# Attention outputs computed transposed, in halves and quarters of the array, in a fused attention and MLP kernel

## The chip, the cores and the metric

One core of a Trainium2 chip runs the whole kernel as one program. The core has five engines with their own instruction streams: TensorE (PE in the profile; its weight loads are shown apart as PEld), VectorE (DVE), ScalarE (ACT), GpSimd (POOL) and SyncE (SP), which issues the DMA transfers. TensorE reads SBUF and writes PSUM, which has eight banks of 512 float32 values in each of 128 partitions. The metric is the time of one execution in microseconds, as the median of several runs; the profile is of one execution.

## The reference

For 4 batches and 8 heads, 768 positions of 48 values:

```
f = 1 / (1 + exp(-f_logit))
for t in range(768):
    state = f[t][:, None] * state + outer(k[t], v[t])     # 48 x 48 per batch and head
    y[t]  = q[t] @ state
x = heads of y side by side                               # [4, 768, 384]
x = x + relu(layernorm(x) * g @ w_ch1) @ w_ch2            # 384 -> 1536 -> 384
x = x + (token MLP over the 768 positions, 768 -> 256 -> 768)
x = x + relu(x @ w_ch1') @ w_ch2'
```

The weights of the MLPs come as float64 and are converted on the chip.

## The kernel before, in words

**Attention in units.** The 768 positions are cut into 6 chunks of 128, and a chunk of one batch is a unit `n` (`c, b = divmod(n, 4)`): 24 units. The function `attention(n)` registers the steps of a unit as named pieces of work. Heads are kept in 4 pairs `p`; the head `r` of a pair (0 or 1) lies in partitions 0 to 47 or 64 to 111 of a tile of 112 (`rows(r)`). The steps, with their names in the order:

- `lt` or `lf`, `lq`, `lv`: the DMA loads of q, k, f and of v; `clamp`, `log`, `scan`, `ek`, `eq`, `qm`, `km`, `tot`: the decay's logarithm, its running sum over the chunk, its exponentials, and q and k multiplied by them.
- `kp`, `kt`: k transposed on TensorE (line 297), and copied out by ScalarE.
- `sc`: the scores, K by Q, for each head with 48 rows of the array (line 312), into the two banks of the PSUM pool `scp`, one for each `r`. `A0`, `A1`: VectorE masks them into SBUF (line 320).
- `y0`, `y1`: the outputs, two pairs of heads each. For every pair one product of Q, 112 x 128, as weights with the carried state of two heads (`state[b]`, 112 x 96 per pair, the two heads' blocks on a diagonal) as 96 moving columns (line 332), if there is a carried state (c > 0); and for every head one of the masked scores, 128 x 128, as weights with V as 48 moving columns (line 335). The result is [128 positions, 384], in a bank of the pool `atp` (three banks).
- `st`: what the chunk adds to the state, for each head 48 columns of the transposed k as weights and 48 of V (line 346); `ste`: VectorE adds it to the state in two instructions, one for each `r` (line 357; ScalarE copies it when c = 0); `std`: GpSimd multiplies the state by the decay (line 350).
- `lna`: ScalarE copies y to `x` with a running sum (line 365); `lnc`, `tp`, `ah`, `al`, `lnv`, `lnr`: the layer norm's product, the transposes (line 418) and their split into a high and a low part, the norm's factor.

**The MLP work around it.** Three units make a step of the first MLP, `mlp(step, ...)`: twelve groups `m<step>.<f>` of nine matmuls of 384 columns (line 449) and twelve groups `m<step>.o<u><g>` of nine (line 479), with ReLU on ScalarE (`h`) and the low part on VectorE (`l`). The weights are loaded (`w<i>.ld`, 384 KB of int32 pairs each), converted by three VectorE instructions (`.a`, `.b`, `.c`) and split (`.h`, `.l`).

**What sets the order.** Each piece has a slot number, and TensorE pieces (`sl.p`) of a slot come behind the others (`sl.e`). Units 9 and later are 8 slots apart, and pieces from slot 77 on are issued by slot: attention first within a slot, then a group of nine matmuls. Pieces of the first 77 slots are issued in an order written out by hand, `ORDER`. An entry such as `0.kp+8` puts 8 matmuls on zeros (256 columns, bf16, `busy`, line 412) ahead of that piece. `POOL` names the pieces that run on GpSimd rather than VectorE. Within an engine the order of issue is the order of execution as written.

After the attention the token MLP and the second channel MLP follow, and last a check of the ranges of the inputs that chooses whether `general_path` runs; here it doesn't run.

Of the kernel before, what the change touches and what calls it, by code (L numbers as in the profile page):

```python
# [7 lines left out]
F32 = mybir.dt.float32  # L8
# [48 lines left out]
    2.lnr 1.al 4.kp w4.b 3.lna 5.lt m0.0 w3.a w2.a 4.kt 3.lnc w2.b 3.tp 4.A0 4.st 3.std 3.ah 5.lv 3.lnv 3.al
    4.y0 4.tot w2.c w3.b w2.h 4.y1 5.clamp w3.c 5.log w2.l m0.1 6.lt w4.c m0.h0 5.scan w4.h 4.lna m0.2 m0.l0
    w4.l 5.ek 4.ste 6.lv 5.eq 5.km m0.4 m0.h2 m0.h1 4.lnc w3.h 5.qm 5.kp m0.h4 w3.l 4.tp 5.kt 5.sc w5.a 4.ah
    m0.l1 5.tot 4.lnv w5.b m0.3 5.A0 4.std 5.A1 0.lnr 4.al 5.y0 m0.h3 w5.c m0.l3 1.lnr w5.h m0.l4 5.y1 w5.l  # L60
    m0.l2 w12.a 5.st 5.lna 7.lt 3.lnr m0.5 w12.b 5.lnc w12.c 5.tp m0.h5 5.ste 4.lnr 5.ah 7.lv 5.lnv 5.al
    5.std w17.ld m0.l5 w12.h m1.0+10 w14.a w13.ld w12.l m1.3 m1.h0 w14.b m1.l0 5.lnr m1.2 w17.a m1.h3 w14.c
    w13.a w14.h w21.ld w13.b m1.4 m1.h2 m1.l3 w14.l w15.ld m1.l2 w13.c m1.1 w17.b w13.h m1.h4 w13.l m1.l4
    m1.5 m1.h1 w15.a w17.c w15.b w17.h m0.o00 m1.l1 m1.h5 w17.l m1.l5 w15.c m0.o20 w16.a w15.h w16.b w16.c
    m0.o10 w15.l w9.ld w16.h w16.l w6.ld 6.clamp m0.o01 w21.a 6.log w21.b w10.ld w21.c m0.o11 6.scan w7.ld
    w21.h w11.ld w9.a 6.ek m0.o21 w21.l m0.r11 6.eq m0.r01 6.qm m1.o00 m0.r21 6.km w11.a 6.kp 6.tot m1.o20
    6.kt w11.b w11.c w9.b w11.h 6.st w11.l m1.o10 w9.c w10.a w20.ld w9.h w9.l m1.o21 w7.a w6.a w6.b m1.o11
    w6.c m1.r21 w8.ld w6.h w6.l 6.sc m1.r11 w10.b m1.o01 6.A1 6.A0 w10.c 6.y0 m1.r01 w10.h w23.ld w10.l m0.6
    w8.a w7.b w8.b m1.9 w8.c m0.h6 m0.l6 w8.h w8.l m1.6 m1.h9 7.clamp 7.log m1.l9 w7.c m0.8 w22.ld m1.h6
    7.scan w7.h w18.ld m1.l6 m1.8 w7.l m0.h8 7.ek m0.l8 7.eq 7.km m1.7 m1.h8 7.qm w20.a m1.l8 7.tot 7.kp  # L70
    m1.h7 w20.b 6.y1 7.kt w20.c w22.a w19.ld w20.h w22.b m0.9 6.lna w20.l 8.lt 6.lnc m0.10 w22.c m0.h9 w23.a
    w22.h w19.a m1.l7 w22.l 7.sc m0.h10 8.lv m0.l9 w19.b s0.ld m0.11 7.A0 w19.c 7.A1 8.clamp w19.h m1.10
    m0.h11 6.ste w19.l 8.log m0.l10 m0.l11 7.y0 6.std m1.h10 8.scan 7.st 7.y1 m1.l10 8.ek w18.a 8.eq 8.km
    6.tp 7.ste 9.lt 7.lna m0.7 6.lnv 8.qm 7.lnc 8.kp 6.ah w18.b 7.tp 8.kt 8.sc 6.al 9.lv 8.tot 7.ah w18.c
    7.lnv 7.al 7.std 8.st m0.h7 8.A0 m1.11 w18.h 7.lnr 8.A1 w18.l m0.l7 8.y0 9.clamp m1.h11 m1.l11 6.lnr
    9.log m0.o02 w23.b 9.scan m0.o12 w23.c 9.ek w23.h s1.ld 9.km m0.o22 9.eq w23.l 9.qm m0.o03 s0.a 9.tot
# [885 lines left out]
```

## Time and profile before

| what | value |
|---|---|
| median of 3 runs | 811.01 us (809.0 to 811.43) |
| the profiled execution | 809.86 us, of which the span from the first to the last instruction is 808.0 us |
| granted TensorE clock over the span | 0.992 |
| TensorE busy | 798.2 us in 5314 matmul instructions |
| VectorE, ScalarE, GpSimd busy | 408.3, 318.1, 212.7 us |
| end of the last output of attention | 393 us |

Busy time is a union of instructions, and those of TensorE overlap, so a share near 100% is to be read together with the times at which instructions start. The granted clock is a share of 2.4 GHz. Times in the timeline are microseconds from the start of the span.

### The profile page before, as it was taken

The page shows a single profiled execution, that of the slowest core. Times are in us where ns is not written, and L with a number is a line of the kernel's source. Part 1 is how long each engine was busy: PE and PEld are TensorE (multiplying, and loading weights), DVE is VectorE, ACT ScalarE, POOL GpSimd, SP SyncE. Part 2 cuts the span into 40 slices and gives each one's busy share as a digit, 9 for nine tenths or more (in the row PEclk, how much of TensorE's full clock was granted, in tenths as well). Part 3 has the DMA queues.
Part 4 walks back from the last instruction along what each step waited for, and adds up shares of the span by engine and source line. Part 5 has one row for each costly group of instructions (what it writes and reads, how often), then busy time and mean ns, then how long its engine had stood idle before and what let it go on. Part 6 is the DMA issues. An engine that isn't in the chain of part 4 may idle for free.

```text
span 808.0 us, 13517 instructions
## 1 busy us (share of the span) xinstructions
PE 798.2 (99%) x5314; PEld 780.8 (97%) x5314; DVE 408.3 (51%) x757; ACT 318.1 (39%) x797; POOL 212.7 (26%) x271
## 2 busy tenths in 40 slices
PE   8999999999999999999999999999999999999996
PEld 7899999999999999999999999999999999999996
DVE  6798896554645655546353352534334343524130
ACT  6664363432433423324043362534434353525020
POOL 4543054333333333322003451111112111212000
PEclk9799999999999999999999999999999999999999
DMA  9535453334544443352152463234333343332000
GB/s 239 203 105 168 118 165 96 124 113 151 147 123 143 119 136 113 118 176 85 40 157 85 130 197 106 79 99 128 108 99 95 101 128 108 82 95 69 30 2 33
DMA packets 42841, 93.19 MB, mean 115 GB/s; under 512 B 4800, under 2 KB 25408, under 8 KB 42768
## 3 DMA queue, kind: packets, MB, share of 16 engines
q1 hardware_dynamic: 42768, 92.23, 38.5%
q8 instruction: 44, 0.72, 0.4%
q14 instruction: 29, 0.24, 0.1%
HBM read 76.48 MB, written 15.73 MB: 114 GB/s over the span
## 4 chain that ended last, share of the span: by engine, by line
PE 96%; DMA 1%; ACT 1%; POOL 0%; issue 0%; SPq 0%; DVE 0%; DVEq 0%; POOLq 0%
PE mo L479 38%; PE mm L449 37%; PE y L335 5%; PE rt L640 3%; PE ht L664 3%; PE sc L312 3%; PE y L332 2%; PE tp L418 2%; PE st L346 1%; DMA first<-in_qkf_t 1%; PE kp L297 1%; DMA xr<-x_d 0%; PE kp L412 0%; POOL first L286 0%; SPq L249 0%
## 5 line engine op out<-in xcount | busy, mean ns | idle before, releaser
L449 PE MATMUL mm<-ah,w1h 128*128 128x384 f32 x576 | 198.0, 344 | 0.2 <-ACT xn L376 0.2
L479 PE MATMUL mo<-w2h,hh 128*128 128x384 f32 x576 | 197.4, 343 | 0.0
L449 PE MATMUL mm<-ah,w1l 128*128 128x384 f32 x576 | 193.1, 335 | 0.0
L479 PE MATMUL mo<-w2h,hl 128*128 128x384 f32 x576 | 193.0, 335 | 0.0
L449 PE MATMUL mm<-al,w1h 128*128 128x384 f32 x576 | 192.8, 335 | 0.0
L479 PE MATMUL mo<-w2l,hh 128*128 128x384 f32 x576 | 192.8, 335 | 0.0
L468 DVE SCALAR_TENSOR_TENSOR hl<-mm,hh 128x384 fp32r<-128x384 f32 x192 | 106.3, 555 | 141.6 <-ACT hh L464 141.4
L464 ACT ACTIVATE hh<-mm 128x384 fp32r<-128x384 f32 x192 | 94.0, 490 | 210.6 <-PE mm L449 210.2
L449 PEld LDWEIGHTS mm<-ah,w1h 128*128 128x128 f32 x576 | 108.2, 188 | 1.7 <-ACT xn L376 0.4
L479 PEld LDWEIGHTS mo<-w2h,hh 128*128 128x128 f32 x576 | 108.2, 188 | 1.6
L449 PEld LDWEIGHTS mm<-al,w1h 128*128 128x128 f32 x576 | 108.3, 188 | 0.2 <-DVE al L435 0.2
L479 PEld LDWEIGHTS mo<-w2l,hh 128*128 128x128 f32 x576 | 108.3, 188 | 0.1
L479 PEld LDWEIGHTS mo<-w2h,hl 128*128 128x128 f32 x576 | 108.1, 188 | 0.0
L449 PEld LDWEIGHTS mm<-ah,w1l 128*128 128x128 f32 x576 | 108.1, 188 | 0.0
L718 POOL TENSOR_TENSOR cs<-cs 128x384 f32<-128x384 f32 x56 | 47.3, 846 | 222.6 <-DVE cs L715 183.4
L435 DVE TENSOR_TENSOR al<-tp,ah 128x384 fp32r<-128x384 f32 x48 | 26.6, 553 | 50.9 <-ACT ah L431 50.8
L431 ACT ACTIVATE ah<-tp 128x384 fp32r<-128x384 f32 x48 | 23.4, 488 | 66.9 <-PE tp L418 66.4
L509 DVE TENSOR_TENSOR xr<-mo,xr 128x384 f32<-128x384 f32 x24 | 13.4, 557 | 68.9 <-PE mo L479 68.9
L335 PE MATMUL y<-V,A 128*128 128x48 f32 x336 | 47.8, 266 | 0.0
L498 DVE SCALAR_TENSOR_TENSOR x<-mo,rs,x 128x384 f32<-128x384 f32 x30 | 18.3, 617 | 55.8 <-PE mo L479 55.8
L335 PEld LDWEIGHTS y<-V,A 128*128 128x128 f32 x336 | 44.1, 191 | 0.3 <-DVE A L320 0.2
L261 POOL TENSOR_SCALAR T<-T 112x512 f32<-112x512 f32 x18 | 27.2, 1513 | 55.1 <-DMA T<-in_qkf_t 55.1
(135 smaller groups left out, 1044.9 us busy)
## 6 DMA issues: line engine op xcount, KB each, us to landing
cs<-in_w SPq DMA_DIRECT2D x48, 384.0 KB, 3.2
sg<-in_w SPq DMA_DIRECT2D x44, 384.0 KB, 3.7
T<-in_qkf_t SPq DMA_DIRECT2D x21, 672.0 KB, 5.3
f_d<-cu SPq DMA_DIRECT2D x32, 192.0 KB, 1.9
wf<-f_d SPq DMA_DIRECT2D x32, 192.0 KB, 2.5
x_d<-x SPq DMA_DIRECT2D x24, 192.0 KB, 1.9
xr<-x_d SPq DMA_DIRECT2D x24, 192.0 KB, 3.3
out<-xr SPq DMA_DIRECT2D x24, 192.0 KB, 1.9
```

The costliest lines, as they stand in the source:

```text
L261: eng("clamp").tensor_scalar(f, f, -43.0, None, op0=ALU.max)
L312: nc.tensor.matmul(t["sc"][r][:, p], t["K"][rows(r), p, :], t["Q"][rows(r), p, :])
L335: nc.tensor.matmul(y[:, D * h:D * h + D], weight(h), v[:, D * h:D * h + D], start=(c == 0), stop=(c == 0 or h % 2 == 1))
L431: nc.scalar.activation(out=ah, in_=src, func=AF.Copy)
L435: nc.vector.tensor_tensor(al, src, ah.bitcast(F32), op=ALU.subtract)
L449: nc.tensor.matmul(ps, w[:, f, k, :], x[:, k, :], start=(i == 0), stop=(i == 8))
L464: nc.scalar.activation(out=hid(f)[0], in_=t[f], func=AF.Relu)
L468: nc.vector.scalar_tensor_tensor(hl, t[f], 0.0, hh.bitcast(F32), op0=ALU.max, op1=ALU.subtract)
L479: nc.tensor.matmul(ps, x, w[:, f, :], start=(f == lo and i == 0), stop=(f == hi and i == 2))
L640: nc.tensor.matmul(t["r"][j][:, :DM], w[:, s, js], t[x, s], start=(s == 0 and i == 0), stop=(s == NCH - 1 and i == 2))
L664: nc.tensor.matmul(ps[:, :DM], w[:, j, js], x[:, j], start=(i == 0), stop=(i == 5))
L718: nc.gpsimd.tensor_tensor(t["u"], t["u"], t["h"], op=ALU.subtract)
```

## The change

Each head's output is computed transposed, [48 values, 128 positions], with what was moving as weights and what was weights as moving columns:

- `outp` takes two PSUM tiles from `scp`, the pool of the scores, one for each `r`. The head with `p % 2 == 0` writes partitions 0 to 63 and that with `p % 2 == 1` partitions 64 to 111, so that two heads lie in the halves of the array's columns. The products with the state use 48 rows at partition 0 or 64 and 64 or 48 columns, a quarter of the array, with Q as 128 moving columns; the products with V use all 128 rows and half of the columns, with the masked scores as 128 moving columns.
- `outp_e` copies the two tiles to SBUF on ScalarE (`yc0`, `yc1`); `outp_t` turns them back by four transposes on TensorE (`yt`) into the bank that `lna` reads.
- The state is stored as 48 columns for each pair, 112 x 192 and no longer 112 x 384; `ste` is one instruction, and `std` works on half as much.
- `st` uses 64 weight columns for the head in the lower half, and moves one slot ahead; `lna` and what follows it move one slot back.
- The heads are dealt out to pairs by `head(p, r)`; the layout on the host and the general path follow.
- `ORDER` and `POOL` are written anew. The matmuls on zeros in `ORDER` are 89, where they were 41: before `0.kp+8 0.y0+3 2.kp+5 3.kp+10 3.y0+5 m1.0+10`; after `0.kp+6 0.sc+9 0.y+6 1.kp+7 1.st+8 1.y+4 0.tp+3 1.tp+3 2.sc+9 2.y+7 2.yt+4 4.y+5 5.y+6 m0.3+12`. In units 4 to 7 it keeps `st` and `y` apart.

```diff
 POOL = set("""
-    1.qm w0.l 2.km 3.clamp w4.l w5.l w12.l 4.clamp w13.l 4.qm w14.l w17.l w7.l 6.qm w19.l w21.l 8.clamp
-    w22.l w23.l 8.km 9.clamp 10.clamp
+    2.clamp 2.qm w2.l w3.l w4.l 4.clamp 4.km w15.l 5.clamp w16.l w6.l w8.l w9.l w19.l 7.km w21.l 9.clamp
+    9.qm 9.km 10.clamp
 """.split())
 ORDER = """
-    0.lf 1.lf 0.lq 0.clamp 0.log 2.lf 1.clamp 1.log 1.lq 0.scan 1.scan 0.ek 1.lv 0.eq 0.km 1.ek 0.lv 1.eq
-    0.qm 0.kp+8 3.lt 0.kt 1.km 0.sc 2.clamp 1.qm 2.log 1.kp 0.A0 0.st 0.A1 2.lq 0.ste 1.tot 0.y0+3 2.scan
-    1.kt 0.tot 2.ek 4.lt 0.y1 3.clamp 2.eq 2.tot 3.log 1.sc 2.qm 0.lna 2.km 1.st 1.A1 2.lv 1.ste 1.A0 w0.ld
...
+    0.lf w0.ld 1.lf 0.lq 0.clamp 0.log w0.a w0.b 2.lf 0.scan 0.lv 1.clamp 0.ek 1.lq w0.c 0.eq 0.km w0.h
+    1.log 0.tot 0.kp+6 w0.l 3.lt 0.qm 0.kt 1.scan 0.sc+9 0.st 2.clamp 1.ek 0.A1 w2.ld 1.eq 0.A0 0.ste 1.lv
+    1.tot 0.y+6 1.qm 2.log 2.lq 3.clamp 1.km 0.yc0 0.yc1 2.scan 1.kp+7 3.log 2.lv 1.sc w5.ld w2.a 2.ek
+    3.scan 0.yt 2.eq w15.ld 1.kt 2.km 3.ek 1.st+8 w14.ld 1.A1 0.std 3.eq 2.kp 1.A0 0.lna 4.lt 2.qm 1.y+4
...
 """.split()
+def head(p, r):
+
+    return 4 * (p // 2) + 2 * r + p % 2
...
-    state = [s1.tile([P2, NP, 2 * D], F32, name=f"state{b}") for b in range(B)]
+    state = [s1.tile([P2, NP * D], F32, name=f"state{b}") for b in range(B)]
...
-        def outp(g, z=0):
-            if g == 0:
-                t["y"] = atp.tile([128, 512], F32, tag="at", name="y")
-                busy(t["y"], z)
-            y = t["y"]
-            v = t["V"]
-            for p in (2 * g, 2 * g + 1):
-                if c:
-                    nc.tensor.matmul(y[:, 96 * p:96 * p + 96], t["Q"][:, p, :], state[b][:, p, :],
-                                     start=True, stop=False)
-                for h in (2 * p, 2 * p + 1):
-                    nc.tensor.matmul(y[:, D * h:D * h + D], weight(h),
-                                     v[:, D * h:D * h + D], start=(c == 0), stop=(c == 0 or h % 2 == 1))
+        def outp(z=0):
+
+            t["yT"] = [scp.tile([128, NP, 128], F32, tag="sc", name="yT") for _ in range(2)]
+            busy(t["yT"][0].rearrange("p a c -> p (a c)"), z)
+            heads = [(p, r, slice(64 * (p % 2), 64 * (p % 2) + (D if p % 2 else 64)))
+                     for p in range(NP) for r in range(2)]
+            if c:
+                for p, r, o in heads:
+                    nc.tensor.matmul(t["yT"][r][o, p // 2], state[b][rows(r), D * p:D * p + o.stop - o.start],
+                                     t["Q"][rows(r), p, :], start=(p < 2), stop=False)
+            for p, r, o in sorted(heads, key=lambda x: x[1]):
+                h = head(p, r)
+                nc.tensor.matmul(t["yT"][r][o, p // 2], t["V"][:, D * h:D * h + o.stop - o.start],
+                                 t["A", r][:, p, :], start=(c == 0 and p < 2), stop=(p > 1))
+
+        def outp_e(r):
+            if not r:
+                t["ys"] = s1.tile([P2, 2, 2, 128], F32, tag="ys", name="ys")
+            nc.scalar.activation(out=t["ys"][:, r], in_=t["yT"][r][:P2, :2], func=AF.Copy)
+
+        def outp_t(z=0):
+            t["y"] = atp.tile([128, 512], F32, tag="at", name="y")
+            busy(t["y"], z)
+            for g in range(2):
+                for r in range(2):
+                    i = 128 * (2 * g + r)
+                    nc.tensor.matmul(t["y"][:, i:i + P2], t["ys"][:, r, g], ident[:P2, :P2], is_transpose=True)
...
-                    h = 2 * p + r
-                    nc.tensor.matmul(ps[rows(r), D * p:D * p + D], kt[:, P2 * p + 64 * r:P2 * p + 64 * r + D],
-                                     v[:, D * h:D * h + D])
+                    h = head(p, r)
+                    w = D if r else 64
+                    nc.tensor.matmul(ps[64 * r:64 * r + w, D * p:D * p + D],
+                                     kt[:, P2 * p + 64 * r:P2 * p + 64 * r + w], v[:, D * h:D * h + D])
...
-            nc.gpsimd.tensor_tensor(state[b], state[b], t["dec"].to_broadcast([P2, NP, 96]), op=ALU.mult)
+            s = state[b].rearrange("p (a c) -> p a c", a=NP)
+            nc.gpsimd.tensor_tensor(s, s, t["dec"].to_broadcast([P2, NP, D]), op=ALU.mult)
...
-            for r in (0, 1):
-                d, new = state[b][rows(r), :, D * r:D * r + D], ps[rows(r)]
-                if c:
-                    nc.vector.tensor_tensor(d, new, d, op=ALU.add)
-                else:
-                    nc.scalar.activation(out=d, in_=new, func=AF.Copy)
+            new = t["st"][:P2, :NP * D]
+            if c:
+                nc.vector.tensor_tensor(state[b], new, state[b], op=ALU.add)
+            else:
+                nc.scalar.activation(out=state[b], in_=new, func=AF.Copy)
...
-                (2, sl.p, lambda z=0: outp(0, z), "y0"), (3, sl.p, lambda: outp(1), "y1"), (4, sl.e, ln_a, "lna"),
-                (3, sl.p, None if last else stat, "st"), (4, sl.e, None if last else stat_e, "ste"),
-                (5, sl.e, None if last else stat_d, "std"), (5, sl.e, ln_c, "lnc"), (6, sl.p, trans, "tp"),
...
+                (2, sl.p, outp, "y"), (3, sl.e, lambda: outp_e(0), "yc0"), (3, sl.e, lambda: outp_e(1), "yc1"),
+                (4, sl.p, outp_t, "yt"), (5, sl.e, ln_a, "lna"),
+                (2, sl.p, None if last else stat, "st"), (3, sl.e, None if last else stat_e, "ste"),
+                (4, sl.e, None if last else stat_d, "std"), (6, sl.e, ln_c, "lnc"), (7, sl.p, trans, "tp"),
```

## Rows read from the trace of the kernel before

**Rows 1.** The page: busy us, share of the span and instructions by engine.

```profile
PE 798.2 (99%) x5314; PEld 780.8 (97%) x5314; DVE 408.3 (51%) x757; ACT 318.1 (39%) x797; POOL 212.7 (26%) x271
```

**Rows 2.** Three stretches: busy us by engine, granted clock, DMA share, GB/s.

```profile
0.00:20.00 20.00, 17.57 (x164) 14.20 (x164) 12.47 (x20) 13.00 (x25) 8.96 (x21) 1.00 0.91 238
...
146.00:325.00 179.00, 179.00 (x1358) 173.56 (x1356) 100.40 (x186) 67.08 (x155) 61.89 (x80) 1.00 0.44 132
...
20.00:31.00 11.00, 10.36 (x68) 9.10 (x68) 7.38 (x12) 5.38 (x15) 5.48 (x5) 0.53 0.81 313
```

**Rows 3.** Timeline of TensorE at a unit's y and state sums: start, length, instruction.

```profile
195.22 0.36 PE L332 MATMUL y<-state,T 112*128 112x96 f32 x2
...
196.48 0.42 PE L479 MATMUL mo<-w2h,hh 128*128 128x384 f32 x1
196.74 0.34 PE L479 MATMUL mo<-w2l,hh 128*128 128x384 f32 x1
...
198.15 0.36 PE L332 MATMUL y<-state,T 112*128 112x96 f32 x2
...
199.51 0.56 PE L346 MATMUL st<-V,kt 128*48 128x48 f32 x16
200.01 0.45 PE L449 MATMUL mm<-ah,w1h 128*128 128x384 f32 x1
200.29 0.34 PE L449 MATMUL mm<-al,w1h 128*128 128x384 f32 x1
```

**Rows 4.** The same timeline, cut within the state sums and within the scores.

```profile
199.51 0.39 PE L346 MATMUL st<-V,kt 128*48 128x48 f32 x8
...
207.24 0.94 PE L312 MATMUL sc<-T 48*128 48x128 f32 x12
```

**Rows 5.** Timeline of TensorE around a unit's scores.

```profile
206.27 0.34 PE L449 MATMUL mm<-al,w1h 128*128 128x384 f32 x1
...
206.97 0.34 PE L449 MATMUL mm<-ah,w1l 128*128 128x384 f32 x1
207.24 1.16 PE L312 MATMUL sc<-T 48*128 48x128 f32 x16
208.33 0.45 PE L449 MATMUL mm<-ah,w1h 128*128 128x384 f32 x1
208.61 0.34 PE L449 MATMUL mm<-al,w1h 128*128 128x384 f32 x1
```

**Rows 6.** Timeline of TensorE around a unit's key transposes.

```profile
203.27 0.55 PE L297 MATMUL kp<-ident,T 112*128 112x112 f32 x4
203.58 0.42 PE L449 MATMUL mm<-ah,w1h 128*128 128x384 f32 x1
203.84 0.34 PE L449 MATMUL mm<-al,w1h 128*128 128x384 f32 x1
```

**Rows 7.** Groups by line, ScalarE, 0 to 400 us: count, busy us, mean ns.

```profile
L365 ACT ACTIVATE x<-y 128x384 f32<-128x384 f32 x24 | 11.7, 489 | 62.9 <-PE y L335 62.0 <-DMA f_d<-cu 0.8
...
L359 ACT ACTIVATE state<-st 48x192 f32<-48x192 f32 x8 | 2.6, 320 | 2.5 <-PE st L346 2.5
```

**Rows 8.** Timeline of ScalarE ahead of that unit's y.

```profile
193.99 0.61 ACT L280 ACTIVATE eq<-T 112x512 f32<-112x512 f32 x1
```

**Rows 9.** Groups by line, 146 to 325 us, VectorE: count, busy us, mean ns.

```profile
L320 DVE TENSOR_TENSOR A<-sc,upper 128x512 f32<-128x512 f32 x20 | 12.9, 684 | 0.2 <-PE sc L312 0.2
...
L357 DVE TENSOR_TENSOR state<-st,state 48x192 f32<-48x192 f32 x20 | 7.1, 356 | 7.9 <-PE st L346 7.8
```

**Rows 10.** Timeline of TensorE in the first 60 us; in brackets idle time and releaser.

```profile
20.64 3.56 PE L335 MATMUL y<-firstv,A 128*128 128x48 f32 x16 [1.24 <-DVE A L320]
...
58.48 1.26 PE L412 MATMUL mm<-zeros 128*128 128x256 bf16 x10
```

More of the change, by code (lines that the diff above doesn't have):

```diff
@@ L57 @@
[L57 to L76, printed above, removed]
@@ new lines @@
+    1.tot 0.y+6 1.qm 2.log 2.lq 3.clamp 1.km 0.yc0 0.yc1 2.scan 1.kp+7 3.log 2.lv 1.sc w5.ld w2.a 2.ek
+    3.scan 0.yt 2.eq w15.ld 1.kt 2.km 3.ek 1.st+8 w14.ld 1.A1 0.std 3.eq 2.kp 1.A0 0.lna 4.lt 2.qm 1.y+4
+    1.ste 2.kt 0.lnc 1.yc0 3.qm 0.tp+3 1.yc1 2.st 0.ah 3.lv 3.km 1.yt 0.lnv 0.al 1.std 3.sc w1.ld 1.lna w2.b
+    w4.ld 3.kp 2.ste 1.lnc 3.kt 3.A1 4.lv 4.clamp 1.tp+3 3.st 3.A0 1.ah w12.ld 0.lnr 1.lnv 1.al 3.y 4.log
+    w1.a w3.ld 2.tot w1.b 3.yc0 5.lv 4.scan 3.yc1 3.ste 2.sc+9 w5.a 4.ek 3.tot 3.yt 4.eq 2.A1 3.std 5.lt
@@ new lines @@
+    3.lna 2.A0 4.km 2.y+7 w5.b 4.kp 2.yc0 4.qm 2.yc1 4.kt 2.yt+4 w5.c 4.sc 3.lnc 2.lna w13.ld w2.c w5.h 3.tp
+    2.lnc w2.h 4.st 4.A0 5.clamp 3.ah 2.tp 3.lnv 4.A1 w2.l 2.ah 3.al 4.y+5 5.log 2.al 3.lnr 4.tot 2.lnv m0.0
+    5.scan 6.lt 4.yc0 4.yc1 w3.a 5.ek 4.yt 4.ste 2.lnr m0.2 4.lna 5.km 6.lv 5.eq 4.lnc 5.kp 5.qm 4.tp 5.kt
+    w3.b 5.sc 4.ah 4.lnv 4.std 4.al 5.st 5.A0 5.tot 1.lnr 5.A1 w3.c 5.y+6 6.clamp w3.h w5.l 6.log w1.c m0.5
+    7.lt 5.ste w3.l 5.yc0 5.yc1 m0.h0 6.scan 5.yt m0.h2 5.lna m0.l2 5.std 7.lv m0.l0 6.ek 5.lnc m0.3+12 6.eq
@@ new lines @@
+    6.km w1.h m0.h5 w1.l 5.tp m0.l5 m0.h3 6.tot m0.1 5.ah w13.a m0.l3 2.std 5.lnv 5.al w13.b m1.3 m0.h1 6.qm
+    w15.a m0.l1 5.lnr m1.5 m1.h3 w15.b m1.l3 4.lnr 6.sc m1.h5 w15.c w13.c w16.ld w15.h m1.0 6.A1 w15.l w13.h
+    m1.l5 w13.l m1.2 m1.h0 w4.a w4.b w4.c m1.1 m1.h2 m1.l0 w4.h w14.a m1.l2 w4.l 6.A0 6.kp m1.h1 w14.b 6.kt
+    6.y m1.l1 w14.c w12.a w14.h w20.ld 6.st w12.b 6.yc0 m0.4 6.yc1 w14.l w17.ld w12.c w16.a w12.h w9.ld 6.yt
+    w16.b m0.h4 m1.4 6.lna w12.l 8.lt w16.c 6.lnc w16.h m0.o10 m1.h4 w17.a m0.l4 w16.l m1.l4 w6.ld m0.o00
@@ new lines @@
+    w17.b w17.c w11.ld w20.a w17.h m0.o20 w20.b 8.lv w17.l w6.a m0.o11 8.clamp w6.b 8.log w6.c m0.o21 w11.a
+    w6.h w11.b m0.r11 w6.l 6.ste m1.o10 w11.c 8.scan w11.h m0.o01 w11.l w20.c m1.o11 7.clamp w21.ld w20.h
+    m0.r01 6.std 7.log m0.r21 w22.ld w20.l m1.o00 7.scan m1.o20 w9.a 7.ek w9.b 8.ek m1.r11 7.km 7.eq m1.o01
+    8.eq w9.c 8.km w7.ld w9.h 6.tp m0.6 m1.r01 6.lnv 7.tot w10.ld 8.tot 8.qm w8.ld m1.o21 7.qm 6.lnr 7.sc
+    w7.a m0.h6 m1.r21 w9.l m0.l6 m1.6 w7.b w7.c 7.A1 w7.h m1.9 m1.h6 w7.l m1.l6 w10.a m1.7 w10.b m1.h9 w10.c
@@ new lines @@
+    m1.l9 w10.h m0.7 m1.h7 w10.l m1.l7 w22.a m1.10 w22.b m0.h7 w22.c w21.a w22.h w21.b 7.kp m1.h10 m0.11
+    w22.l 7.kt w21.c 7.A0 w18.ld w21.h 7.st m0.h11 m1.l10 w21.l 7.y m0.l7 w19.ld w8.a w8.b w23.ld m0.9 w8.c
+    7.yc0 9.lt 7.yc1 w18.a w8.h w18.b m0.l11 w8.l 8.sc m0.h9 7.ste w18.c m1.8 8.A1 7.std w18.h 9.lv 8.A0
+    s0.ld w18.l m0.8 m1.h8 m1.l8 9.clamp m0.l9 8.y w19.a 9.log w19.b s1.ld w19.c m0.h8 m1.11 9.scan w19.h
+    m0.l8 w19.l 9.ek m0.10 9.eq w23.a s2.ld m1.h11 9.qm m1.l11 m0.o22 6.ah m0.h10 w23.b 6.al 9.km m0.o12
@@ L80 @@
+    m0.l10 s3.ld w23.c m0.o02 s0.a w23.h 9.tot w23.l s1.a m0.o13 s0.b s1.b s1.c m0.o03 s0.c m0.r13 s0.h
+    m0.o23 m0.r03 m0.d1 m0.d0 7.yt m0.r23 8.kp 8.yc0 m0.d2 m1.o12 8.yc1 7.lna 10.lt 8.kt 7.lnc 9.sc 8.yt
+    9.A0 m1.o13 8.lna 9.A1 8.lnc 9.y m1.r13 10.clamp m1.d1 10.log 8.st 7.tp 8.ste 10.lv m1.o02 7.ah 10.scan
+    7.lnv 7.al 8.std 10.ek m1.o03 10.eq 7.lnr 8.tp m1.r03 9.kp 8.lnv m1.d0 m1.o22 8.ah 9.kt 8.al 9.st m1.o23
 """.split()
@@ L312, in scores @@
                     nc.tensor.matmul(t["sc"][r][:, p], t["K"][rows(r), p, :], t["Q"][rows(r), p, :])
-        def weight(h):
-            return t["A", h % 2][:, h // 2, :]
         def scores_e(g):
@@ L364, in ln_a @@
             t["nm"] = sm.tile([128, 1], F32, tag="nm", name="nm")
-            nc.scalar.activation(out=x, in_=t["y"][:, :DM], func=AF.Copy, accum_out=t["nm"])
+            nc.scalar.activation(out=x.rearrange("p (i a c) -> p i a c", i=4, a=2),
+                                 in_=t["y"].rearrange("p (i a c) -> p i a c", i=4, a=2)[..., :D], func=AF.Copy,
+                                 accum_out=t["nm"])
             nc.scalar.activation(out=t["nm"], in_=t["nm"], func=AF.Copy, scale=-1.0 / DM)
@@ L399, in attention @@
                 (0, sl.e, lambda: scores_e(0), "A0"), (0, sl.e, lambda: scores_e(1), "A1"),
-                (2, sl.p, lambda z=0: outp(0, z), "y0"), (3, sl.p, lambda: outp(1), "y1"), (4, sl.e, ln_a, "lna"),
-                (3, sl.p, None if last else stat, "st"), (4, sl.e, None if last else stat_e, "ste"),
-                (5, sl.e, None if last else stat_d, "std"), (5, sl.e, ln_c, "lnc"), (6, sl.p, trans, "tp"),
-                (7, sl.e, lambda: transposes_h(n // 3, n % 3, t["tp"]), "ah"),
-                (7, sl.late, lambda: transposes_l(n // 3, n % 3, t["tp"]), "al"),
-                (8, sl.e, ln_v, "lnv"), (9, sl.e, ln_r, "lnr")):
+                (2, sl.p, outp, "y"), (3, sl.e, lambda: outp_e(0), "yc0"), (3, sl.e, lambda: outp_e(1), "yc1"),
+                (4, sl.p, outp_t, "yt"), (5, sl.e, ln_a, "lna"),
+                (2, sl.p, None if last else stat, "st"), (3, sl.e, None if last else stat_e, "ste"),
+                (4, sl.e, None if last else stat_d, "std"), (6, sl.e, ln_c, "lnc"), (7, sl.p, trans, "tp"),
+                (8, sl.e, lambda: transposes_h(n // 3, n % 3, t["tp"]), "ah"),
+                (8, sl.late, lambda: transposes_l(n // 3, n % 3, t["tp"]), "al"),
+                (9, sl.e, ln_v, "lnv"), (10, sl.e, ln_r, "lnr")):
             if f:
@@ L873, in general_path @@
                     x = gx.tile([128, DM], F32, tag="x", name="gx_x")
-                    nc.sync.dma_start(out=x, in_=x_d[b, bass.ds(c, 1), :, :].rearrange("a t d -> (a t) d"))
+                    src = x_d[b, bass.ds(c, 1), :, :].rearrange("a t (p r e) -> (a t) p r e", p=NP, r=2)
+                    dst = x.rearrange("t (g r a e) -> t g a r e", g=2, r=2, a=2)
+                    for p in range(NP):
+                        nc.sync.dma_start(out=dst[:, p // 2, p % 2], in_=src[:, p])
                     bs = gx.tile([128, 6], F32, tag="bs", name="gbs")
@@ L931, in layout @@
         "v_n": nat(v),
-        "v_t": v.reshape(B, NP, 2, S, D).transpose(0, 2, 4, 1, 3),
+        "v_t": v.reshape(B, 2, 2, 2, S, D).transpose(0, 2, 5, 1, 3, 4).reshape(B, 2, D, NP, S),
         "g_rep": np.broadcast_to(moe_g_ln, (128, DM)),
```

10 lines of the change are left out of this document (1 added, 9 removed).

## The prediction

> **What bounds the kernel now.** Read the busy times by engine first: TensorE is busy for 798.2 of 808.0 us, VectorE for half of that [rows 1]. A busy share alone doesn't say that the engine is full, since its matmuls overlap, so look next at one stage: from 146 to 325 us it is busy for all 179.00 us at a granted clock of 1.00 while VectorE works 100 and ScalarE 67 us [rows 2]. Then take the timeline and read starts, not durations: a matmul of the weights starts 0.175 us after the one before ((206.97 - 206.27)/4 [rows 5]), and whatever stands between two of these pushes the end out by its own length. So a microsecond less of TensorE in this stage is a microsecond less of the run, and the sum below is one of start-to-start times. The first 60 us are another case: there TensorE waits for its inputs, and the order fills waits with matmuls on zeros.
>
> **What an attention instruction costs.** A float32 product is two instructions. Half of y is twelve, with 128 weight columns and 96 or 48 moving ones. It runs from 195.22 to 196.48 and slows the next matmul by 0.085 (196.74 - 196.48 - 0.175): 1.345 us, 0.112 each, and groups of 48 columns are no faster than those of 96, so y is paced by its weights [rows 3]. Scores use half of the rows, and two go side by side: 12 take 0.94 us and 16 take 1.16, 0.11 a pair. State sums use half of the columns, 48 of weights and 48 moving: 8 take 0.39 us and 16 take 0.56, 0.043 a pair [rows 3 to 5]. A pair thus costs some 0.0009 us per column of its longer side. Changing between whole and divided array costs too: ahead of scores 207.24 - 206.97 - 0.175 = 0.095, behind them 208.61 - 208.33 - 0.175 = 0.105, and of the block's 1.09 us the 8 pairs are 0.88 and 0.21 is filling and emptying: 0.41 in all [rows 5].
>
> **Before, per unit n with a carried state.** The first half of y 1.345; second half and state sums from 198.15 to 200.01, and 0.105 behind (200.29 - 200.01 - 0.175): 3.31 us [rows 3].
>
> **After, per unit.**
> - State products: 16 instructions on quarters (48 rows, 64 columns), 128 moving columns. No row shows quarters. Four at once: 4 x 0.11 = 0.44 us. Two at once, as scores and state sums: 0.88. I take 0.44: pairs form along rows (scores) and along columns (state sums), and the new order of heads puts four different quarters in a row.
> - Products with V: 16 on column halves, paired: 8 x 0.11 = 0.88, where the old form takes 16 x 0.11 = 1.76.
> - Entering, filling, leaving: 0.41 once. Between quarters and halves there is another change, with no row of its own: nothing to 0.41. I take 0.15, the 0.10 ahead of the state sums (198.15 + 1.26 to 199.51 [rows 3]) and a little filling.
> - State sums follow in the same halves, with 64 weight columns for one head of two: 8 x 0.058 = 0.47, no entry of their own.
> - Four transposes of 112 columns are those of kp: 203.27 to 203.58, and 203.84 - 203.58 - 0.175 behind: 0.395 us [rows 6].
>
> Together 0.44 + 0.88 + 0.41 + 0.15 + 0.47 + 0.395 = 2.745: **0.56 us less**. Units 20 to 23 have no state sums: before 2 x 1.345, after 2.275, 0.41 less. In units 4 to 7 the order keeps y and state sums apart, which costs 0.41 a second time: 0.15 less. Units 0 to 3 have no state products: 1.76 + 0.085 for y and 0.10 + 0.50 + 0.105 for the sums before, 0.88 + 0.41 + 0.47 + 0.41 + 0.395 after: no gain. In the full stage (6 and 7, 8 to 19, 20 to 23): 2 x 0.15 + 12 x 0.56 + 4 x 0.41 = **8.7 us less**.
>
> A rule speaks against this. The Trainium skill, TensorEngine Tiling (Tiling Modes, Key Properties), says that a change of tiling mode, though not one of tile, drains the engine. The trace agrees, with 0.095 and 0.10 us ahead of scores and state sums. The page has no price; by it alone the block of y has two such drains where the old one had none, some 0.2 us a unit, which the terms above hold already.
>
> **Other engines.** ScalarE gains two copies of 256 columns a unit; from 320 ns for 192 and 489 for 384 [rows 7] that is 0.376 us each, 18 us in all, behind TensorE's matmuls of the weights. The chain of y, copies and transposes gets longer: from the end of y to the transposes TensorE has the state sums and one group of nine, 0.47 + 9 x 0.175 = 2.05 us, and the copies need 0.75. The exponentials ahead of y end at 193.99 + 0.61, before y starts [rows 3, 8]. That leaves 1.3 us of cover; without it each unit waits. VectorE adds the state in one instruction of 192 columns, not in two of 356 ns [rows 9]; GpSimd's product of the state halves. Both are covered by the same matmuls before and after, so nothing. The general path is compiled and not run: nothing.
>
> **The first 60 us.** Both score banks now also hold y's transposed outputs, so the scores of the next unit wait for the copies. The order has 89 matmuls on zeros where it had 41; ten take 1.26 us, some 0.11 each [rows 10]: 48 more are 5.3 us, less 0.3 for units 4 and 5: +5.0. On the other side, from 20 to 31 us the granted clock is 0.53 [rows 2]: TensorE stands nearly throughout at 1.2 GHz, the lower of its two levels (1.2 and 2.4). It had idled 1.24 us for VectorE's A, and its 16 instructions of y then took 3.56 us [rows 10]. Zeros spread more evenly may keep the clock up; half of some 10.4 us of busy time is 5.2 to win. It can also be worse: two weight loads of 393 KB are now issued ahead of unit 2's q and k, at 238 GB/s [rows 2] 1.65 us each. Ends: -0.2 and +8.3. I take +2.5, half of the dip gone.
>
> **Sum.** -8.7 + 2.5 = -6.2 us on the profiled execution's 809.86 (808.0 of span and 1.86 around it): 803.7. The median shown, 811.01, lies 1.15 above that execution; with half of it carried over, 804.
>
> **The rivals.**
> - *The start eats the gain* (slower). Place: units 0 to 5 and the two score banks. If nothing else fills the time of A (2 x 0.684 [rows 9]) and of the copies (0.75), each unit costs TensorE 2.1 us, 12.7 in all; against 8.7 that is +4.0: 814. It decides from 8.7 + 2.4 = 11.1 us on. For it: shared banks, more zeros, a longer chain to the first MLP input. Against: in the order key and state transposes, other units' work and the first MLP groups stand in these gaps.
> - *Quarters don't go four at a time.* With 0.88 for them a unit gains 0.12, units 20 to 23 lose 0.03 and units 4 to 7 lose 0.29: 1.4 - 0.1 - 0.6 = 0.7 won in the full stage, and at the start +2.5 and another 0.9: +2.7, about 813. For it: two at once is all that rows show, and the two passes of a product stand next to each other, so that three other quarters' first passes have to overtake one's second. Against: scores do overtake, since 16 instructions are 8 pairs with no single one ahead. The Trainium skill, TensorE: Matmul & The Clock Gate (Part 3, What overlaps and what doesn't), has matmuls start strictly in program order, which would make this the case; the pairs of the scores don't bear that out.
> - *The transposes wait for ScalarE.* If it comes later than the 1.3 us of cover, by its two exponentials just then, TensorE may stand 0.5 us in each of units 8 to 23: 8.0 of the 8.7 are gone, and with +2.5 the run is at 812, no change. Against: the rows of ScalarE above.
>
> **How the numbers follow.** The forecast, four at a time and a start of at most +6, has 0.62; the start 0.13, quarters 0.18 (part of it three at a time, some 2 us slower than the forecast), transposes 0.07. The best end, no cost for the change between quarters and halves (16 x 0.15) and -0.2 at the start, is 11.3 less: 798.6. The forecast's own range is 798.5 to 809; with the rivals 798 to 813.5. A difference of 0.3%, 2.4 us, is about what a measurement of this kernel can tell from none. Faster by more: the forecast and some of the quarters, 0.66. Slower: most of the start and half of the quarters, 0.19. Within: 0.15.
>
> **What would show it.** In the timeline of a late unit: the 16 state products in some 0.6 us (four abreast) or 1.0 (two), products with V and state sums in one block of some 1.4 us behind them, and four transposes in 0.4 us with no idle time ahead. In the first 40 us: the granted clock from 20 to 31 us, and whether idle time stands ahead of scores. The prediction is wrong if the quarters take 0.9 us or more, if transposes wait, or if the stretch without waits begins over 6 us later for the same work done.

## The result and the profile after

The changed kernel takes 800.65 us, the median of 4 runs (798.34 to 803.12), and the kernel before 811.22 (4 runs, 809.0 to 813.37): a ratio of 0.987, 95% interval 0.9831 to 0.991. That is 10.6 us less, where 7 were forecast; the range, 798 to 813.5, holds it, and the forecast was "faster". The profiled execution of the changed kernel took 798.34 us with a span of 796.6.

The page of the changed kernel, busy time by engine, answers to [rows 1]:

```profile
PE 785.7 (99%) x5618; PEld 758.5 (95%) x5618; DVE 398.5 (50%) x745; ACT 332.3 (42%) x841; POOL 208.9 (26%) x267
```

TensorE is still the full engine. ScalarE has risen by 14 us and VectorE has fallen by 10; neither has come near to the span. The three stretches of [rows 2], in the same columns:

```profile
0.00:20.00 20.00, 18.49 (x183) 14.73 (x184) 13.29 (x25) 12.32 (x23) 5.73 (x17) 1.00 0.92 252
20.00:31.00 11.00, 9.50 (x130) 7.61 (x127) 9.22 (x16) 8.49 (x25) 6.54 (x9) 1.00 0.96 303
146.00:325.00 179.00, 179.00 (x1520) 170.10 (x1519) 100.86 (x187) 78.13 (x182) 66.00 (x83) 1.00 0.47 139
```

The late stage has no gap on TensorE, as before, so there a difference is read from start times. From 20 to 31 us the granted clock is 1.00, where [rows 2] has 0.53: the whole dip is gone, and the forecast had counted half of it.

The timeline of TensorE at a unit with a carried state, which answers to [rows 3] (start, length, instruction):

```profile
189.90 0.34 PE L499 MATMUL mo<-w2h,hl 128*128 128x384 f32 x1
190.16 0.65 PE L335 MATMUL yT<-T,state 48*64 48x128 f32 x16
190.75 1.09 PE L339 MATMUL yT<-A,V 128*64 128x128 f32 x16
191.67 0.62 PE L364 MATMUL st<-V,kt 128*48 128x48 f32 x16
192.22 0.44 PE L499 MATMUL mo<-w2h,hh 128*128 128x384 f32 x1
192.50 0.34 PE L499 MATMUL mo<-w2l,hh 128*128 128x384 f32 x1
...
195.47 0.55 PE L353 MATMUL y<-ident,ys 112*128 112x112 f32 x4
195.78 0.42 PE L469 MATMUL mm<-ah,w1h 128*128 128x384 f32 x1
196.04 0.34 PE L469 MATMUL mm<-al,w1h 128*128 128x384 f32 x1
```

From start to start (0.175 us is the pace of the weight matmuls): entering 190.16 - 189.90 - 0.175 = 0.085; state products 0.59; products with V 0.92; state sums 0.55; leaving 192.50 - 192.22 - 0.175 = 0.105. That is 2.25 us, and the transposes take 195.78 - 195.47 + 0.085 = 0.395: 2.645 in all, against 3.31 before. A unit gains 0.665 us, where 0.56 was forecast.

The same timeline, cut off at 190.25, 190.38 and 190.49, counts the state products that have started by then:

```profile
190.16 0.33 PE L335 MATMUL yT<-T,state 48*64 48x128 f32 x4
...
190.16 0.44 PE L335 MATMUL yT<-T,state 48*64 48x128 f32 x8
...
190.16 0.55 PE L335 MATMUL yT<-T,state 48*64 48x128 f32 x12
```

Each step of 0.11 us adds four: the quarters do go four at a time.

Units 20 to 23, without state sums, in the same view:

```profile
359.96 0.34 PE L469 MATMUL mm<-ah,w1l 128*128 128x384 f32 x1
360.23 0.65 PE L335 MATMUL yT<-T,state 48*64 48x128 f32 x16
...
361.83 0.44 PE L469 MATMUL mm<-ah,w1h 128*128 128x384 f32 x1
362.11 0.34 PE L469 MATMUL mm<-al,w1h 128*128 128x384 f32 x1
```

0.095 + 1.60 + 0.105 + 0.395 = 2.195 us against 2.69: 0.495 less, forecast 0.41. ScalarE's copies, in its timeline (in brackets the idle time and what ended it):

```profile
191.45 0.82 ACT L345 ACTIVATE ys<-yT 112x256 f32<-112x256 f32 x2 [1.53 <-PE yT L339]
```

The copies end at 192.27, 3.2 us ahead of the transposes at 195.47. The first 60 us, as the waits of TensorE: who waits for what, us in total, times, longest:

```profile
PE warm L572 <- DVE zeros L542: 1.1, 1, 1.1
PE sc L432 <- ACT ys L345: 1.0, 1, 1.0
PE yT L432 <- DVE A L323: 0.7, 3, 0.3
PE st L364 <- DMA V<-in_v_n: 0.4, 1, 0.4
```

The second and third line are matmuls on zeros. They have been given the bank that the next real piece will write, so they stand behind the same release as that piece, here ScalarE's copy and VectorE's masking, and don't fill the time until it. From 60 to 400 us this view has no row at all: neither transposes nor scores wait for ScalarE.

Last, how far the MLP is at 60 us: the first MLP's weight matmuls of the stretch 0 to 60 us, their busy time and count, in the changed kernel, then in a second profiled execution of the same kernel (c_changed_again, below):

```profile
0.00:60.00 60.00, 12.29 (x63) 1.00 0.66 189
```

```profile
0.00:60.00 60.00, 10.30 (x53) 1.00 0.68 188
```

The kernel before had done 56. At 0.175 us each the start is thus 1.2 us ahead of before in one execution and 0.5 behind in the other, so it costs nothing that two executions agree on. The full stage gives 12 x 0.665 + 4 x 0.495 + 2 x 0.25 (units 6 and 7, the forecast's 0.15 and the same 0.1 more) = 10.5 us, and that is the difference of the medians.

The traces also give this gain directly. From the start of the 57th weight matmul of the first MLP to that of its last, the 1728th, it is 397.90 us before, and 387.07 and 386.95 in the two executions after: 10.8 and 10.95 us less. About a microsecond is lost again behind it: from that last start to the end it is 350.0 us before, 351.0 and 351.3 after. No run tells why.

A start that costs nothing hides two large terms. Over the whole span the granted clock of the kernel before was 0.987 to 0.999 in the 53 executions on record beside the experiments, and its time went with it: 804.1 to 806.3 us in the five at 0.998 or more, 810.9 to 812.2 in the nine at 0.988 or less. The lower clock thus goes with 5 to 6 us. The changed kernel had 0.997 to 0.999 in all ten of its executions. Next to the kernel before at that clock it gains about 5.5 us, not 10.6, so the rest of its start should cost some 4 to 5. This is a relation between executions, not an experiment, and in which stretch the clock fell is known of the profiled one alone (20 to 31 us).

### The profile page after: what moved, and what is told of

Read it like the earlier page. It is cut to its first block, busy times and chain, and to the rows that moved or that the text cites. A ratio compares the mean times of both kernels' runs of the same rounds, so it can differ in the third digit from the quotient of the medians.

```text
span 796.6 us, 14109 instructions
## 1 busy us (share of the span) xinstructions
PE 785.7 (99%) x5618; PEld 758.5 (95%) x5618; DVE 398.5 (50%) x745; ACT 332.3 (42%) x841; POOL 208.9 (26%) x267
## 4 chain that ended last, share of the span: by engine, by line
PE 93%; DMA 3%; DVE 1%; SPq 1%; ACT 1%; issue 0%; POOL 0%; DVEq 0%
PE mo L499 38%; PE mm L469 37%; PE ht L684 3%; PE rt L660 3%; PE sc L318 3%; DMA T<-in_qkf_t 3%; PE yT L339 3%; PE tp L438 2%; PE yT L335 1%; PE y L353 1%; PE st L364 1%; PE kp L303 1%; DMA xr<-x_d 1%; SPq L255 0%; POOL T L267 0%
## 5 line engine op out<-in xcount | busy, mean ns | idle before, releaser
L741 ACT ACTIVATE cs<-cs 128x384 f32<-128x384 f32 x56 | 31.0, 553 | 9.4 <-POOL cs L738 9.3
L323 DVE TENSOR_TENSOR A<-sc,upper 128x512 f32<-128x512 f32 x48 | 31.0, 685 | 7.4 <-PE sc L318 7.2
```

What stands on the lines that cost most here:

```text
L323: nc.vector.tensor_tensor(a, t["sc"][g], upper.rearrange("p (o c) -> p o c", o=1).to_broadcast([128, NP, 128]), op=ALU.mult)
L741: nc.scalar.activation(out=t["u"], in_=t["u"], func=AF.Abs, accum_out=wlow[:, i:i + 1])
```

## The experiments

The theory at the outset: units gain because quarters run four abreast and V's products two abreast, the start costs little, and nothing waits. Against it stood, first, that the order of heads is what makes them pair, and secondly that the start or a wait of the transposes takes part of the gain. Ratios are against the kernel before, in runs on the same chip.

**The changed kernel again** (c_changed_again), as the base for the others.

> The changed kernel once more, beside the two others: 800 to 801 us. If the spread between executions comes from the start (loads that land sooner or later), its profile shows another number of matmuls of the weights by 60 us than the first one, and from 146 us on the same pace.

800.52 us, 6 runs (798.86 to 801.38), ratio 0.989 (0.987 to 0.9909). The gain stands; a comparison below should be made with this 800.5 and not with the 798.34 of the first profile.

**Quarters issued two by two** (e1_quarters_in_pairs).

```
-                for p, r, o in heads:
+                for p, r, o in sorted(heads, key=lambda x: (x[0] % 2, x[0])):
```

> The changed kernel with its state products issued so that only the two row halves of one column half follow each other (pairs 0, 2, 1, 3). If four quarters at once are what makes the state block 0.59 us in a late unit: it becomes about 1.0 us, 0.4 more in each of units 6 to 23, +6 to +8 us, about 808 us and a ratio to the kernel before near 0.996. If it is short for another reason (64 weight columns where there were 128): the block stays under 0.7 us and the time at 801.

801.88 us, 8 runs, ratio 0.9906 (0.9876 to 0.9935). Its timeline, first cut at 193.7 and then whole, and the groups by line up to 193.7:

```profile
193.62 0.34 PE L335 MATMUL yT<-T,state 48*64 48x128 f32 x4
...
193.62 0.67 PE L335 MATMUL yT<-T,state 48*64 48x128 f32 x16
194.22 1.09 PE L339 MATMUL yT<-A,V 128*64 128x128 f32 x16
...
L335 PE MATMUL yT<-T,state 48*64 48x128 f32 x2 | 0.3, 321 | 0.0
L335 PE MATMUL yT<-T,state 48*48 48x128 f32 x2 | 0.3, 307 | 0.0
```

Next to the base of another sitting the time says little (the intervals of the two ratios overlap); the row does. 0.60 us, against 0.59 without the edit. Of the first four starts two have 48 weight columns, so they belong to the other half of the columns, though the first eight instructions of the program now all have 64 and name only two quarters. The order of heads was the reason given for "four at once"; it isn't the reason. An instruction whose quarter is free starts ahead of one whose quarter is busy. So the sentence on the kernel before, that within an engine the order of issue is the order of execution, doesn't hold across quarters. (The order meant is that of kernel.py; the trace doesn't list it.) The Trainium skill, TensorE: Matmul & The Clock Gate (Part 3, What overlaps and what doesn't), has matmuls start strictly in program order; for products in different parts of the array the 0.60 us contradict it.

**V's products not in pairs** (e2_v_not_paired): all heads of one column half, then those of the other.

```
-            for p, r, o in sorted(heads, key=lambda x: x[1]):
+            for p, r, o in sorted(heads, key=lambda x: (x[1], x[0] % 2, x[0])):
```

> The changed kernel with the products of V issued half by half, so that the two column halves no longer alternate. If pairing of halves carries the gain: the V block goes from 0.92 to about 1.8 us, 0.85 more in each of 18 full-stage units and part of it at the start, +15 to +19 us, about 818 us, slower than the kernel before. If the gain comes from the start or from shorter weights: no more than 2 us slower than the changed kernel.

801.77 us, 10 runs, ratio 0.9906 (0.988 to 0.9932). The timeline:

```profile
193.56 1.13 PE L339 MATMUL yT<-A,V 128*64 128x128 f32 x16
194.48 0.62 PE L364 MATMUL st<-V,kt 128*64 128x48 f32 x16
```

0.92 us again. The order inside a block of sixteen doesn't matter here either.

**State products in halves** (e9_state_in_halves): 112 rows instead of 48, so that only the columns are divided.

```
-  nc.tensor.matmul(t["yT"][r][o, p // 2], state[b][rows(r), D * p:...], t["Q"][rows(r), p, :], ...)
+  nc.tensor.matmul(t["yT"][r][o, p // 2], state[b][:, D * p:...], t["Q"][:, p, :], ...)
```

> The changed kernel with its state products on all 112 rows and half of the columns, so no longer on quarters; each then also adds the other head's state (the outputs differ, the number of instructions doesn't). If quarters running four at a time make the block 0.59 us, whatever the order of issue: it becomes about 1.0 us, +0.4 in each of units 6 to 23, about 808 us. If columns alone were enough: 801 as with quarters.

807.22 us, 10 runs, ratio 0.9979 (0.9961 to 0.9997). The timeline:

```profile
192.34 1.13 PE L335 MATMUL yT<-T,state 112*64 112x128 f32 x16
193.26 1.08 PE L339 MATMUL yT<-A,V 128*64 128x128 f32 x16
194.14 0.61 PE L364 MATMUL st<-V,kt 128*64 128x48 f32 x16
```

The state products take 0.92 instead of 0.59. Times 20 units that is 6.6 us, and the kernel is 6.7 slower than its base, which was measured on another chip; in the traces the stretch from the 57th to the last weight matmul is 392.60 us, 5.6 more than the base's. So about three quarters of the gain hang on the quarters, and what a unit loses is lost at the end of the run. The rows also price the change from quarters to halves, which has none here. In quarters the block is 0.59 - 4 x 0.11 = 0.15 over its pace and V's 0.92 - 0.88 = 0.04; in halves the two are 0.92 - 0.88 = 0.04 and 0.88 - 0.88 = 0. The change costs 0.15 us, the value of the forecast. That is also what the Trainium skill, TensorEngine Tiling (Tiling Modes, Key Properties), leads one to look for: a change of mode drains the engine.

**V's products over the whole array** (e10_v_whole_array): 128 weight columns and all rows, one at a time.

```
-  nc.tensor.matmul(t["yT"][r][o, p // 2], t["V"][:, D * h:D * h + o.stop - o.start], ...)
+  h = min(h, 5)
+  nc.tensor.matmul(t["yT"][r][:, p // 2], t["V"][:, D * h:D * h + 128], ..., start=True, stop=True)
```

> The changed kernel with its products of V on the whole array, 128 weight columns each, in place of 64 or 48 in a half; the outputs of the state products are overwritten and two heads in four land in the wrong place, the number of instructions is the same. If the halves running two at a time carry the gain: the V block goes from 0.92 to about 1.8 us and a change of tiling comes on top, +0.9 to +1.2 in 18 full-stage units, 817 to 823 us, slower than the kernel before. If the transposed form by itself or the start carried it: under 804.

821.69 us, 4 runs, ratio 1.0156 (1.0122 to 1.019): slower than before the change. The timeline:

```profile
182.71 2.05 PE L340 MATMUL yT<-A,V 128*128 128x128 f32 x16
184.69 0.67 PE L365 MATMUL st<-V,kt 128*64 128x48 f32 x16
```

1.98 us instead of 0.92. Turning the outputs round, with its copies and transposes, gains nothing by itself: with V's products undivided, and the state products still in quarters, the kernel is 12 us slower than before (821.69 - 809.86). The division of the array has to pay for it.

**No matmuls on zeros** (e4_no_zeros): every `+k` out of the order.

```
-    1.log 0.tot 0.kp+6 w0.l 3.lt 0.qm 0.kt 1.scan 0.sc+9 ...
+    1.log 0.tot 0.kp w0.l 3.lt 0.qm 0.kt 1.scan 0.sc ...
```

> The changed kernel with none of the 89 matmuls on zeros of its order (the 56 at the very start stay). If they hold the clock up at the start: the granted clock between 20 and 40 us falls below 0.8 and the time is 801 to 806 us. If they are only delay: the clock stays at 1.00 and the time falls to 796 to 799 us.

800.16 us, 6 runs, ratio 0.9892 (0.9858 to 0.9925). Its two early stretches:

```profile
0.00:20.00 20.00, 15.88 (x122) 12.50 (x124) 12.65 (x24) 11.25 (x20) 5.45 (x16) 0.84 0.93 224
20.00:31.00 11.00, 10.20 (x98) 7.93 (x94) 7.33 (x13) 7.44 (x21) 2.93 (x3) 0.67 1.04 293
```

The zeros do hold the clock: without them it is 0.84 and 0.67. Over the span it is 0.989 or 0.990 in all six executions. The time is the same without them. The likely reading is that they take as work and as waits what they give in clock, since in the kernel before a span clock of 0.989 or 0.990 goes with 809.7 to 812.8 us, by the medians some 5 more than one of 0.998 or 0.999. This run alone can't tell that from a start that hangs on the loads, which keep the DMA engines busy throughout (0.93 and 1.04), so that neither counts.

**Zeros in the kernel before** (e6_before_with_zeros), where it waited 1.24 us for A [rows 10].

```
-    0.std 2.kp+5 1.y0 2.kt ...
+    0.std 2.kp+5 1.y0+12 2.kt ...
```

> The kernel before with 12 matmuls on zeros ahead of unit 1's first half of y, where TensorE idled 1.24 us, and nothing else changed. If the dip of the clock at 20 to 31 us is what the start of the changed kernel gained: the granted clock there rises from 0.53 to over 0.9 and the time falls by 3 to 5 us, to 806 to 808. If the start is bound by loads and VectorE: under 1 us.

The ratio is 0.9991 (0.9957 to 1.0025), 10 runs: no difference can be told. But its executions are of two kinds: six at a granted clock of 0.998 to 1.00 over the span take 805.8 to 806.6 us, four at 0.987 to 0.990 take 811.2 to 814.6. The profiled one, of 814.62 us, is of the second kind; two early stretches:

```profile
20.00:31.00 11.00, 11.00 (x117) 9.57 (x115) 7.31 (x12) 5.68 (x18) 6.74 (x6) 0.79 0.94 354
31.00:40.00 9.00, 8.06 (x85) 6.98 (x85) 8.35 (x15) 6.30 (x17) 5.26 (x6) 0.90 0.26 81
```

Here the clock is 0.79 instead of 0.53 from 20 to 31 us, and 0.90 from 31 to 40 us: the dip is shallower and longer and not gone. The six at the full clock took about what was expected of a kernel without the dip, 806 to 808 us, while of the 25 executions of the kernel before beside them three reached 0.998. The ratio of all ten decides nothing, but the two kinds put the price of the lower clock at some 5 us or more once again.

**Transposes one slot earlier** (e3_turned_back_at_once).

```
-                (4, sl.p, outp_t, "yt"), (5, sl.e, ln_a, "lna"),
+                (3, sl.p, outp_t, "yt"), (5, sl.e, ln_a, "lna"),
```

> The changed kernel with the four transposes one slot earlier from unit 9 on, with only the state sums between the products and them. If ScalarE's two copies need 0.75 us after the last product: idle time of 0.2 to 0.4 us stands ahead of the transposes, +3 to +6 us, 804 to 807. If the first copy runs while the products of the second tile do: under 0.1 us of idle time in units with state sums, and no change of the time that can be measured; units 20 to 23, without state sums, wait about 0.4 us each.

800.91 us, 4 runs, ratio 0.9894 (0.9861 to 0.9926), the base within its spread. One group of nine still stands ahead of the transposes (without the edit there are two), so the expectation's case of state sums alone wasn't reached. In a unit without state sums there is nothing but that group:

```profile
347.58 0.44 PE L499 MATMUL mo<-w2h,hh 128*128 128x384 f32 x1
...
349.07 0.34 PE L499 MATMUL mo<-w2h,hl 128*128 128x384 f32 x1
349.25 0.55 PE L353 MATMUL y<-ident,ys 112*128 112x112 f32 x4
```

The transposes start 0.18 us after the last of the nine, without a gap: 1.67 us from the first matmul behind V's products (349.25 - 347.58) is cover enough.

**State sums in a slot of their own** (e11_state_sums_apart), which adds one more change of the array.

```
-                (2, sl.p, None if last else stat, "st"), (3, sl.e, ... stat_e, "ste"),
+                (3, sl.p, None if last else stat, "st"), (4, sl.e, ... stat_e, "ste"),
```

> The changed kernel with the state sums one slot later from unit 9 on, so behind a group of matmuls of the weights and no longer right behind the products of V. If a change between whole and divided array costs about 0.4 us a block: 11 units pay it once more, +3.5 to +4.5 us, about 805 us. If following in the same tiling saves nothing: 801.

803.63 us, 4 runs, ratio 0.993 (0.9905 to 0.9955), 3.1 over its base. The timeline:

```profile
192.79 1.09 PE L339 MATMUL yT<-A,V 128*64 128x128 f32 x16
193.81 0.44 PE L499 MATMUL mo<-w2h,hh 128*128 128x384 f32 x1
194.09 0.34 PE L499 MATMUL mo<-w2l,hh 128*128 128x384 f32 x1
...
195.30 0.34 PE L499 MATMUL mo<-w2h,hl 128*128 128x384 f32 x1
195.57 0.67 PE L364 MATMUL st<-V,kt 128*64 128x48 f32 x16
196.16 0.44 PE L469 MATMUL mm<-ah,w1h 128*128 128x384 f32 x1
196.44 0.33 PE L469 MATMUL mm<-al,w1h 128*128 128x384 f32 x1
```

The sums alone: 0.095 to enter (195.57 - 195.30 - 0.175), 0.59, 0.105 to leave. Less their pace of 0.47, entering, filling and leaving cost 0.32 us. The forecast took 0.41, from the scores [rows 5], which divide the rows; a division of the columns is 0.09 cheaper. Apart, V's products and the state sums take 1.02 + 0.105 + 0.095 + 0.59 + 0.105 = 1.915 us, and together 0.92 + 0.55 + 0.105 = 1.575 in the base: 0.34 a unit.

**Fewer changes** (e7_fewer_switches, then e13_fewer_switches_2): the transposes stand beside those of k, and the state sums have 48 columns for both heads, added by two instructions. In the first, the later pieces moved one slot on, and so the layer norm's transposes no longer stood beside the scores; the second keeps them there.

```
-                    w = D if r else 64
+                    w = D
...
-            new = t["st"][:P2, :NP * D]
...
+            for r in (0, 1):
+                d, new = state[b][rows(r)], t["st"][rows(r), :NP * D]
...
-                (4, sl.p, outp_t, "yt"), (5, sl.e, ln_a, "lna"),
+                (5, sl.p, outp_t, "yt"), (6, sl.e, ln_a, "lna"),
```

> The changed kernel with two edits meant to save TensorE time: the transposes of y one slot later, side by side with the key transposes of the next unit (with the layer norm's steps behind them), and state sums with 48 weight columns for both heads (VectorE then adds them in two instructions). By the sum of start-to-start times: 0.085 us a unit for one entry and exit less in 14 units, and 0.1 us in 20 units for the shorter loads: 2 to 3 us less, about 798. If the state sums are not paced by their loads or a later step waits: 800 to 802.

800.11 us, 6 runs, ratio 0.9888 (0.9861 to 0.9915): no gain that can be told from its base. In the trace the full stage did gain: from the 57th to the last weight matmul of the first MLP it is 385.49 us, 1.5 less than in the base, but the 57th starts at 62.86 us and in the base at 60.59.

> The changed kernel with state sums of 48 weight columns for both heads, and the transposes of y one slot later beside the key transposes of the next unit, but the transposes behind the layer norm left beside the scores. By start-to-start times 0.1 us in each of units 4 to 19 and 0.085 in some 10 units less: 2 to 2.5 us below the changed kernel. If the layer norm's steps, now in one slot, come late: idle time ahead of its transposes and no gain.

797.96 us, 5 runs (797.63 to 798.55), ratio 0.9862 (0.9841 to 0.9882). This is the fastest of all, 2.6 below its base, whose six runs begin at 798.86. The timeline of the second:

```profile
190.85 0.53 PE L364 MATMUL st<-V,kt 128*48 128x48 f32 x16
191.31 0.44 PE L500 MATMUL mo<-w2h,hh 128*128 128x384 f32 x1
...
196.12 0.55 PE L353 MATMUL y<-ident,ys 112*128 112x112 f32 x4
196.51 0.55 PE L303 MATMUL kp<-ident,T 112*128 112x112 f32 x4
196.82 0.42 PE L470 MATMUL mm<-ah,w1h 128*128 128x384 f32 x1
197.08 0.34 PE L470 MATMUL mm<-al,w1h 128*128 128x384 f32 x1
```

The size is as expected, the reason only in part. The state sums take 0.46 instead of 0.55, which is 16 x 0.09 = 1.4 us. The two sets of transposes side by side take 197.08 - 196.12 - 0.175 = 0.785, and apart they took 2 x 0.395: nothing is saved there. From the 57th to the last weight matmul of the first MLP it is 385.21 us, 1.7 less than in the base: the 1.4 and 0.3 more. The rest of the difference doesn't belong to the edit's sum: this execution's 57th starts 2.1 us earlier (58.46), and the stretch behind the last is 1.3 us longer. Why start and end move so stays open.

## Why the prediction was right, step by step

**The bound.** TensorE's start times set the end. e9 and e11 confirm it with two costs: 20 x 0.33 = 6.6 by the units of the trace and 6.7 in the time, and about 0.34 x 11 = 3.7 and 3.1.

**State products in quarters, 0.44 us.** Right in size; the trace has 0.59 up to V's products, of which 0.15 is the change to halves. The reason given, four different quarters in a row, is wrong: in e1 they aren't in a row, and the block takes 0.60 all the same. The rival "two at once", 18 in 100, had the price of its block right, 0.88 against 0.92 in e9, which forces it and loses three quarters of the gain.

**V's products in halves, 0.88, the transposes, 0.395, and the state sums, 0.47.** Measured 0.92, 0.395 and 0.55 with what they leave to be emptied.

**Entering, filling and leaving, 0.41.** Mis-sized. What a unit's block has over its terms is 2.25 - 0.44 - 0.88 - 0.47 = 0.46, less 0.15 for the change to halves 0.31; e11's sums alone say 0.32. The nearest row was that of the scores, and it was of another division. This is the 0.1 us a unit by which the full stage gave 10.5 and not 8.7.

**The start, +2.5.** Mis-sized too: about 0. The forecast had +5.0 for the zeros against up to 5.2 for the dip and took half of the dip; it went whole, and its own other end, -0.2, is what came. The executions of the kernel before put the lower clock at 5 to 6 us; what the zeros cost no run measured alone, since e4 takes away zeros and clock together. The rival in which the start eats the gain fell: it priced waits of 2.1 us in each of six units, 12.7 us, and those of the four rows shown come to 3.2 us, of which 1.1 ahead of `warm` stood there before too. Between executions of one kernel the start moves by some 2 us (63 and 53 weight matmuls at 60 us); why, no run separates.

**No wait of the transposes.** Right, with the cover too small: two groups of nine stand in it and not one, and ScalarE's copies end 3.2 us ahead where 1.3 was forecast. There is no row in the waits, and in e3 no gap behind one group of nine. VectorE and GpSimd cost nothing, as forecast.

With the two terms put right the sum is 809.86 - 10.5 + 0 = 799.4, and the kernel measured 800.65 and 800.52; the microsecond lost behind the first MLP, which no term held, is about the difference. Both terms were too dear, so the run came out under the forecast of 804. One size, that of the quarters, was right for a wrong reason, and that was luck.

## What to carry to other kernels

Products on a quarter of the array ran four at a time here and those on a half two; quarters in place of halves were worth 0.33 us for sixteen instructions, and turning the operands round without dividing V's products (e10) would have lost 12 us. Price the change of division from a row with the same division, rows or columns, and keep the pieces of one division in one block. In a stage where the engine has no gap, such sums of start times can be trusted to a microsecond; in a stage that waits for loads, they can't: here the start moved by some 2 us between executions of one kernel. And when a kernel's executions differ, set their times beside their granted clocks before reading a median (e6).

## What the runs showed that had not been expected

Within a block of sixteen float32 instructions, two to a product, the order in the program made no difference: 0.60 us against 0.59 in quarters (e1), 0.92 against 0.92 in halves (e2). A matmul on zeros that is given the bank of the piece behind it waits for the same release: it stood 1.04 us behind ScalarE's copy, and nothing was filled. State sums with weights of 48 columns for both heads take 0.46 us, with 64 for one of the two 0.55.
